# Six low-word roundings moved from ScalarE to VectorE, another order of the weight halves, and more of the output stored by column halves

## The chip, the cores and the metric

The program runs on one core of a Trainium2 chip. The metric is the device time of one execution in microseconds, as a median over timed runs. The engines are named as in the profile: PE is TensorE (matmuls; PEld its weight loads), DVE is VectorE, ACT is ScalarE, POOL is GpSimd and SP is the engine that issues the DMAs here.

## The reference, cut to what matters

```
x (8 batches, 8 heads, 512 tokens, 64), state (8, 8, 32, 64)
1. attention  a  = softmax(x @ state^T / 8);   xread = a  @ state
              a2 = softmax(state @ x^T / 8);   sread = a2 @ x
   out = concat([xread, sread])  ->  8 * 544 rows of 512
2. feed-forward  g = silu(rows @ w_in), rows = g @ w_out       (512 -> 2048 -> 512)
3. soft mixture  logits = rows @ phi                            (32 slots)
   dispatch = softmax over the rows; slot inputs = dispatch^T @ rows
   8 experts (relu(in @ w1[e]) @ w2[e]), 4 slots each
   out = softmax over the slots @ slot outputs                  (4352 x 512)
```

`moe_w_in` and `moe_w_out` are float64: each number is two 32-bit words, a high and a low one, and the kernel makes float32 numbers of them on the chip.

## The kernel before, in words

**Work and stages.** Eight batches of 512 tokens are the blocks k = 0 to 7; the 256 rows that belong to the states of all batches are block 8 (`NB`). For a block, `hid` makes sixteen tiles h (j = 0 to 15) with six fp32r matmuls each; fq = j // 4 says which fourth of the 2048 hidden columns a tile belongs to. For it the block's state rows are multiplied into that fourth of w_in (`wb`, the tiles wbp and wb), and the attention weights are the other operand (`ar`). ACT applies silu into a tile g, DVE transposes it into `blk_t[k]`, and `logits` multiplies it with `w2p`, which is the product of w_out's fourth and phi. There are six g buffers, and `logits` frees them. `s_dTg` (tiles S) gathers the slot sums of a block later. After block 8 the slot inputs go through w1 (tiles f) and w2 (tiles so), and `out_tiles` makes the output (tiles o).

**Conversion.** w_in and w_out^T come in sixteen halves of 1 MB (`raw`): four fourths of each, two halves per fourth, in the order of the list `halves`: both halves of a fourth of w_in, then both of the same fourth of w_outT. Eight halves are requested at the start (four in each of two large buffers), the others as `conv` frees a place in the second buffer. `conv` turns a half into float32 in four steps: ACT `activation` Prelu on the high words; ACT `activation` Identity on the low words into `part` (the low words are every second word of the raw half); DVE shift by three in place; POOL integer add of the two. `win_half` converts a half of w_in; `wo_half` a half of w_outT, and after the second one two small matmuls (w2ps, w2q) make `w2p` of that fourth. In the first block the calls are: `win_half` of fourth 0 around the first attention, `wo_half` of fourth 0, and then for each next fourth both halves of w_in and both of w_outT.

**Order of the work.** Nothing is issued when the Python code runs: a recorder keeps all operations, and `schedule` plans them with costs that it gives each one (`cost`). At each step an engine takes, among the operations that can start within `LOOK` of the earliest, the one with the smallest `prio`: its place in the recorded order plus a shift plus an entry of the table `RANK`. PE has a rule more: it stays among operations of its present tiling mode (full 128x128 against row- or column-tiled) as long as the best of them is not behind by more than `STAY` or `KEEP`. The planned order of each engine is what is issued. DMAs are operations on SP and are ordered the same way.

**The end.** w1 and w2 (32 MB) come in 32 loads (`load_w`) into buffers as they become free. w2 is loaded by column halves: eight loads for columns 0 to 255, then eight for 256 to 511. As soon as the first column half of the slot outputs is there, `out_tiles` makes columns 0 to 255 of the first `HALVES` = 3 batches and stores them (512 KB each, rows of 1 KB); later, batches 0 to 2 get their second halves, and batches 3 to 7 and the states' rows are made with 512 columns at a time and stored in rows of 2 KB, the states' rows last (two DMAs from 32 partitions each).

```
        if ch == 0:

            for q in range(HALVES):
                out_tiles(q, slice(0, 256), sets[0])
    for q in range(NB + 1):
        out_tiles(q, slice(256 if q < HALVES else 0, 512), sets[(q + HALVES) % 2])
```

Of the kernel before, what the change touches and what calls it, by code (L numbers as in the profile page):

```python
# [25 lines left out]

BY_PE = (NB,)

WIN = (2, 6)
WIN8 = (0, 2)  # L30

# [6 lines left out]

EVICT = 100

HALVES = 3

# [1 line left out]


RANK = {
    ("0", "ACT", "activation", "acc", 0): 8,
    ("0", "ACT", "activation", "part", 12): 8,  # L50
    ("0", "ACT", "activation", "win", 3): 13,
    ("0", "ACT", "copy", "wb", 2): 71,
    ("0", "DVE", "tensor_scalar", "acc", 0): -9,
    ("0", "DVE", "tensor_scalar", "asm", 3): 120,
    ("0", "DVE", "tensor_tensor", "wb", 0): 459,
    ("0", "DVE", "tensor_tensor", "wb", 3): 126,
    ("0", "DVE", "transpose", "blk", 7): -36,
    ("0", "DVE", "transpose", "s", 4): -40,
    ("0", "PE", "matmul", "lg", 5): 58,
    ("0", "PE", "matmul", "lg", 7): -81,  # L60
    ("0", "PE", "matmul", "wq", 3): -125,
    ("0", "PE", "transpose", "eT", 2): 59,
    ("0", "PE", "transpose", "srT", 1): -75,
    ("7", "DVE", "tensor_reduce", "m", 0): 434,
    ("7", "PE", "matmul", "h", 0): -39,
    ("7", "PE", "matmul", "h", 8): -120,
    ("7", "PE", "matmul", "lg", 5): 30,
    ("7", "PE", "matmul", "wbp", 1): 76,
    ("8", "DVE", "scalar_tensor_tensor", "fin", 0): 68,
    ("8", "PE", "matmul", "S", 3): 155,  # L70
    ("8", "PE", "matmul", "f", 9): 165,
    ("8", "PE", "matmul", "f", 13): 120,
    ("8", "PE", "matmul", "h", 17): 166,
    ("8", "PE", "matmul", "lg", 6): 120,
    ("8", "PE", "matmul", "so", 4): 51,
    ("8", "PE", "transpose", "gt", 8): 71,
    ("8", "PE", "transpose", "hT", 3): -134,
    ("8", "PE", "transpose", "lT", 0): 120,
    ("m", "ACT", "activation", "m", 0): 698,
    ("m", "DVE", "tensor_scalar", "asm", 1): 28,  # L80
    ("m", "PE", "matmul", "S", 2): -150,
    ("m", "PE", "matmul", "h", 5): -324,
    ("m", "PE", "matmul", "lg", 8): -96,
    ("m", "PE", "matmul", "lg", 9): -50,
    ("m", "PE", "transpose", "lT", 0): 416,
}


# [35 lines left out]
class Recorder:  # L124
# [90 lines left out]
    def cost(self, op, eng, what, outs, ins, kwargs):  # L215

        def n(v):
            r = 1
            for s, c in list(v.ap)[1:]:
                r *= c  # L220
            return r

        ps = bass.MemoryType.PSUM
        most = max(n(v) for v in outs + ins)
        pin, pout = any(v.space == ps for v in ins), any(v.space == ps for v in outs)
        strided = any(list(v.ap)[-1][0] > 1 and list(v.ap)[-1][1] > 1 for v in outs + ins)
        if eng == PE:
            lhs, rhs = kwargs.get("lhsT"), kwargs.get("rhs")
            if what == "transpose":
                op.mode, op.tail = FULL, 0.2  # L230
                op.cost += 0.11
                return
            rows, cols = list(lhs.ap)[0][1], n(lhs)
            op.mode = (128 if rows > 64 else 64 if rows > 32 else 32, 128 if cols > 64 else 64 if cols > 32 else 32)
            N = n(rhs)
            if op.mode == FULL:
                split = rhs.dtype == F32R
                op.cost += N / 2.4e3 + 0.0212 if split else max(0.2, 4 * N / 2.4e3 + (0.021 if N > 256 else 0.04))
                op.tail = 0.165
            else:  # L240
                tiles = (128 // op.mode[0]) * (128 // op.mode[1])
                m = 2 * len(op.calls)
                op.cost = max(m / tiles * 2 * N / 2.4e3, m * 0.0135) + (0.07 if tiles == 16 else 0.0068 * tiles)
                op.tail = 0.165
        elif eng == ACT:
            f = kwargs.get("func")
            base = 0.833e-3 * most
            if f in (AF.Abs, AF.Sign, AF.Relu):
                lat = base + (0.26 if pin else 0.29)
            elif len(ins) > 1 and most < 1024:  # L250
                lat = base + (0.258 if pin else 0.285)
            else:
                lat = base + (0.16 if pin else 0.205)
            if kwargs.get("accum_out") is not None:
                op.cost, op.tail = lat + 0.096, 0.0
            else:
                op.cost, op.tail = lat - 0.105, 0.105
            op.mode = {AF.Exp: "e", AF.Silu: "s", AF.Tanh: "es"}.get(f)
        elif eng == DVE:
            sb = [kwargs[x] for x in ("in0", "in1") if x in kwargs and kwargs[x].space == bass.MemoryType.SB]  # L260
            fast = not pin and not pout and what in ("tensor_scalar", "tensor_copy")
            op.port = len(sb) > 1 or fast
            if what == "transpose":
                lat = 0.165 + most / 0.96e3
            elif what == "reciprocal":
                lat = 0.165 + max(0, most - 4) * 6.7e-3
            elif fast:
                lat = 0.262 + most / 1.92e3
            else:
                lat = (0.205 if pin and len(ins) > 2 else 0.155) + most / 0.96e3  # L270
            op.cost, op.tail = lat - 0.08, 0.0 if fast else 0.08
        elif eng == POOL:
            lat = 0.2 + most * 2.135e-3
            if most == 1024:
                lat = 2.39 if outs[0].dtype == F32R else 1.94
            op.cost, op.tail = lat - 0.042, 0.042
        else:
            b = 4
            for s, c in list(outs[0].ap):
                b *= c  # L280
            op.bytes = b
            op.cost = 0.42
# [19 lines left out]
    def schedule(self):  # L302
# [37 lines left out]
        while n_left:  # L340
            best = None
            for e in avail:
# [20 lines left out]
                    continue  # L363
                t_e = min(c[0] for c in cands)
                cands = [c for c in cands if c[0] <= t_e + LOOK[e]]
                pick = min(cands, key=lambda c: (c[1].prio, c[0]))
                if e == PE and mode is not None:
                    near = [c for c in cands if (c[1].mode == FULL) == (mode == FULL)]
                    if near:
                        near = min(near, key=lambda c: (c[1].prio + SAME * (change(c[1]) > 0.2), c[0]))  # L370
                        if near[1].prio <= pick[1].prio + (STAY if mode == FULL else KEEP):
                            pick = near
                if best is None or pick[0] < best[0]:
# [79 lines left out]
        return lambda *a, **k: self._rec.record(self._eng, what, call, a, k)  # L453


LOOK = {PE: 0, DVE: 0.302, ACT: 0.098, POOL: 0.05, SP: 0.0}
DMA_RATE = 405e3
FULL = (128, 128)
STAY, KEEP, SAME = 60, 60, 30


@with_exitstack
def tile_state_attention_soft_moe(
# [65 lines left out]

    raws = [unit("blk", [4, 1024, 2], f"raw{i}", U32) for i in range(2)]  # L530
    n_raw = [0]
    halves = [(kind, f, x) for f in range(4) for kind in ("win", "wo") for x in range(2)]

    def raw_at(n):
        return raws[0][:, n] if n < 4 else raws[1][:, n % 4]
# [7 lines left out]
        src = {"win": w_in, "wo": w_outT}[kind][fq, half].bitcast(U32)  # L543
        nc.sync.dma_start(out=raw_at(n).rearrange("p a b -> p (a b)"), in_=src)

    def conv(raw, dst, r):


        v = raw.rearrange("p (c f) b -> p c f b", f=dst.shape[-1])
        lo, hi, d, r = v[..., 0], v[..., 1], dst.bitcast(U32), r.bitcast(U32)  # L550
        nc.scalar.activation(out=dst, in_=hi.bitcast(F32), func=AF.Prelu, scale=2.0**-112, alpha=2.0**32)
        nc.scalar.activation(out=r, in_=lo, func=AF.Identity, scale=2.0**-29, bias=ulps)
        nc.vector.tensor_scalar(out=d, in0=d, scalar1=3, scalar2=None, op0=ALU.logical_shift_left)
        nc.gpsimd.tensor_tensor(out=d, in0=d, in1=r, op=ALU.add)

# [23 lines left out]

    def wo_half(fq, half):  # L580

        n = 4 * fq + 2 + half
        conv(raw_at(n), acc[:, 2 * half:2 * half + 2], share(half))
        if n >= 4:
            next_raw()
        if half == 0:
# [11 lines left out]
        nc.scalar.mul(out=w2p[:, fq].rearrange("p i s -> p (i s)"), in_=p[:, 0:128], mul=-0.5)  # L598

    def win_half(fq, half):  # L600
        n = 4 * fq + half
        conv(raw_at(n), win_t[fq][:, :, 256 * half:256 * half + 256], share(half))
        if n >= 4:
            next_raw()

# [49 lines left out]
    def a_split(b):  # L655
# [4 lines left out]
        p = at[b, "sc"]  # L660
        for h2 in range(2):
            nc.scalar.copy(out=e[:, 0, h2, :], in_=p[h2])
            nc.vector.transpose(out=s[:, 0, h2, :], in_=e[:, 0, h2, :])
        nc.vector.reduce_max(out=sm[:, 0:2], in_=e[:, 0], axis=AX.X)
        nc.vector.tensor_scalar(out=sm[:, 2:4], in0=sm[:, 0:2], scalar1=-SCALE, scalar2=None, op0=ALU.mult)
        at[b, "tm"] = tm = rot.tile([128, 32, 2], F32, tag="tm", name=f"tm{b}")
# [477 lines left out]
    win_half(0, 1)  # L1144
    a_soft1(0)
    wb(0)
    a_soft2(0)
    a_soft3(0)
    wo_half(0, 0)
    wo_half(0, 1)  # L1150
    load_xT(1)
    a_eT(0, 0)
    a_eT(0, 1)
# [8 lines left out]
    for k in range(NB):  # L1162
# [4 lines left out]
        for j in range(16):  # L1167
# [6 lines left out]
                logits(*divmod(4 * k + fq - 1, 4))  # L1174
                nc.shift = 0
            if k == 0 and i == 0 and fq < 3:
                win_half(fq + 1, 0)
                win_half(fq + 1, 1)
                wo_half(fq + 1, 0)
                wo_half(fq + 1, 1)  # L1180
            if k > 0:
                if j == 1:
                    nc.shift = -FIRST
# [191 lines left out]
    for ch in range(2):  # L1375
# [16 lines left out]
        nc.vector.tensor_copy(out=sor[:, 256 * ch:256 * ch + 256], in_=p[:, 0:256])  # L1392
        if ch == 0:

            for q in range(HALVES):
                out_tiles(q, slice(0, 256), sets[0])
    for q in range(NB + 1):
        out_tiles(q, slice(256 if q < HALVES else 0, 512), sets[(q + HALVES) % 2])
    for k in range(NB + 1):

        lo, hi = WIN8 if k == NB else WIN if k else (4, 4)
# [51 lines left out]
```

## Time and profile before

| what | value |
|---|---|
| median of 3 runs | 467.94 us (467.29 to 468.88) |
| the profiled execution | 466.55 us, its span 464.0 us |
| PE busy | 414.1 us, 89% of the span |
| DVE, ACT, POOL busy | 296.3, 279.6, 135.5 us |
| granted PE clock, mean | 0.984 |
| HBM read and written | 79.37 MB and 12.06 MB |

The span is the time from the first to the last instruction in the trace; the profiled execution's own time holds 2.55 us around it. Times in the rows below are microseconds from the start of the span, mean durations of one instruction nanoseconds.

### The profile page before, as it was taken

The page shows a single profiled execution, that of the slowest core. Times are in us where ns is not written, and L with a number is a line of the kernel's source. Part 1 is how long each engine was busy: PE and PEld are TensorE (multiplying, and loading weights), DVE is VectorE, ACT ScalarE, POOL GpSimd, SP SyncE. Part 2 cuts the span into 40 slices and gives each one's busy share as a digit, 9 for nine tenths or more (in the row PEclk, how much of TensorE's full clock was granted, in tenths as well). Part 3 has the DMA queues.
Part 4 walks back from the last instruction along what each step waited for, and adds up shares of the span by engine and source line. Part 5 has one row for each costly group of instructions (what it writes and reads, how often), then busy time and mean ns, then how long its engine had stood idle before and what let it go on. Part 6 is the DMA issues. An engine that isn't in the chain of part 4 may idle for free.

```text
span 464.0 us, 12243 instructions
## 1 busy us (share of the span) xinstructions
PE 414.1 (89%) x5334; PEld 261.6 (56%) x5334; DVE 296.3 (64%) x519; ACT 279.6 (60%) x488; POOL 135.5 (29%) x75
## 2 busy tenths in 40 slices
PE   1177789999999999999999999999999998899870
PEld 0044456667757766865775776676476784334420
DVE  0876774797787797789778778779942424221280
ACT  3799998758586495585757759568457413011170
POOL 2464577224124133222412313421056410000000
PEclk9999999999999999999999999999999999899995
DMA  8998740510602412142060251212385899999898
GB/s 317 425 429 330 297 167 1 184 59 35 229 2 92 150 80 93 54 175 93 1 229 1 92 171 59 93 47 93 131 324 182 311 375 420 398 426 424 324 331 305
DMA packets 19845, 92.20 MB, mean 199 GB/s; under 512 B 1616, under 2 KB 5072, under 8 KB 11344
## 3 DMA queue, kind: packets, MB, share of 16 engines
q1 hardware_dynamic: 19792, 91.43, 51.3%
q8 instruction: 41, 0.67, 0.6%
q14 instruction: 12, 0.10, 0.1%
HBM read 79.37 MB, written 12.06 MB: 197 GB/s over the span
## 4 chain that ended last, share of the span: by engine, by line
PE 78%; ACT 7%; DMA 6%; DVE 3%; POOL 2%; issue 1%; SPq 0%; DVEq 0%; POOLq 0%
PE h L427 41%; PE S L427 8%; PE lg L427 7%; PE wbp L427 6%; DMA place<-in_w_dram 4%; PE f L427 3%; PE sc L427 2%; ACT part L427 2%; DMA xT<-in_xT_dram 2%; PE eT L427 2%; PE sr L427 2%; PE o L427 1%; PE sib L427 1%; POOL win L427 1%; PE dT L427 1%
## 5 line engine op out<-in xcount | busy, mean ns | idle before, releaser
L427 PE MATMUL h<-ar,wb 128*128 128x512 f32 x768 | 190.2, 400 | 2.0 <-ACT g L427 2.0
L427 PEld LDWEIGHTS h<-ar,wb 128*128 128x128 f32 x768 | 141.7, 190 | 41.3 <-issue 6.9
L427 DVE STREAM_TRANSPOSE blk<-g 128x512 f32<-128x512 f32 x128 | 86.4, 693 | 39.1 <-ACT g L427 38.9
L427 ACT ACTIVATE g<-h 128x512 f32<-128x512 f32 x100 | 59.3, 602 | 77.9 <-PE h L427 56.8
L427 POOL TENSOR_TENSOR wb<-wf,wb 128x512 fp32r<-128x512 f32 x28 | 36.6, 1307 | 152.4 <-ACT wf L427 90.2
L427 PE MATMUL wbp<-win,ss 64*32 64x512 f32 x512 | 34.0, 610 | 10.0 <-POOL win L427 10.0
L427 PEld LDWEIGHTS lg<-g,w2p 128*32 128x32 f32 x1152 | 29.1, 109 | 18.9 <-issue 5.7
L427 ACT CAST wb<-wbp 128x512 fp32r<-128x512 f32 x64 | 34.7, 604 | 7.2 <-PE wbp L427 7.2
L427 PE MATMUL lg<-g,w2p 128*32 128x128 f32 x1152 | 39.0, 276 | 0.0
L427 PE MATMUL S<-blk,dT 32*32 32x512 f32 (+1 forms) x1040 | 38.5, 598 | 0.4 <-ACT dT L427 0.4
L427 POOL TENSOR_TENSOR s<-s,tm 128x1024 f32<-128x1024 f32 x12 | 23.3, 1939 | 33.4 <-DVE tm L427 33.4
L427 DVE TENSOR_TENSOR wb<-wbp,wb 128x512 fp32r<-128x512 f32 x36 | 24.3, 681 | 6.4 <-ACT wb L427 6.3
L427 ACT ACT_TABLE_LOAD x21 | 26.9, 1283 | 1.1 <-PEq L1443 0.7
L427 POOL TENSOR_TENSOR win<-win,part 128x1024 uint32<-128x1024 uint32 x8 | 19.4, 2436 | 24.9 <-DVE win L427 8.6
L427 POOL TENSOR_TENSOR wlo<-win,whi 128x1024 fp32r<-128x1024 f32 x8 | 18.9, 2389 | 16.5 <-ACT whi L427 16.5
L427 POOL TENSOR_TENSOR acc<-acc,part 128x1024 uint32<-128x1024 uint32 x8 | 20.5, 2559 | 9.3 <-ACT part L427 4.6
L427 DVE SCALAR_TENSOR_TENSOR g<-thb,h 128x512 f32<-128x512 f32 x28 | 18.2, 677 | 5.7 <-ACT thb L427 5.7
L427 PEld LDWEIGHTS wbp<-win,ss 64*32 64x32 f32 x512 | 7.5, 106 | 24.8 <-POOL win L427 11.8
L427 PE MATMUL h<-whi,rd 128*128 128x512 f32 x64 | 20.7, 404 | 0.0
L427 PEld LDWEIGHTS S<-blk,dT 32*32 32x32 f32 (+1 forms) x1040 | 13.0, 103 | 13.2 <-issue 8.6
L427 DVE SCALAR_TENSOR_TENSOR acc<-acc,m,S 128x512 f32<-128x512 f32 x28 | 19.1, 742 | 2.0 <-PE S L427 2.0
L427 ACT ACTIVATE part<-raw,ulps 128x1024 uint32<-128x1024 uint32 x16 | 20.0, 1256 | 0.0
(151 smaller groups left out, 563.7 us busy)
## 6 DMA issues: line engine op xcount, KB each, us to landing
place<-in_w_dram SPq DMA_DIRECT2D x17, 1024.0 KB, 9.4
blk<-in_w_dram SPq DMA_DIRECT2D x13, 1024.0 KB, 10.0
raw<-in_w_in_dram SPq DMA_DIRECT2D x8, 1024.0 KB, 7.8
xT<-in_xT_dram SPq DMA_DIRECT2D x8, 1024.0 KB, 5.2
raw<-in_w_outT_dram SPq DMA_DIRECT2D x8, 1024.0 KB, 7.8
xk<-in_xk_dram SPq DMA_DIRECT2D x8, 1024.0 KB, 5.0
blk<-in_w_out_dram SPq DMA_DIRECT2D x6, 1024.0 KB, 4.8
wo_f<-blk SPq DMA_DIRECT2D x6, 512.0 KB, 2.7
```

Source lines behind the costliest of these rows:

```text
L427: made = [call(*args, **kwargs) for call, args, kwargs in op.calls]
```

## The change

The low words of six of the sixteen halves (numbers 4, 6, 8, 10, 12, 14 of the list) are rounded by a DVE `tensor_scalar` in place of ACT's `activation`. The halves come in another order: fourths 0 and 1 of w_in, fourth 0 of w_outT, then in turn a fourth of w_in and one of w_outT, with w_outT's last fourth at the end; requests and conversion calls follow it. In the first block's attention DVE transposes the scores from PSUM in place of ACT's copy. At the end `HALVES` becomes a list: the first column halves of batches 0 to 6 and of the states' rows are made and stored as soon as the first half of the slot outputs is there, then the second halves in the same order, and batch 7 last with 512 columns at a time. The planner gets other costs, other `LOOK`, `STAY`, `KEEP` and `SAME`, and another `RANK` table, which holds SP entries too. The diff, with the table cut to the entries for SP:

```diff
+RAW = [("win", 0), ("win", 1), ("wo", 0), ("win", 2), ("wo", 1), ("win", 3), ("wo", 2), ("wo", 3)]
+
+LOW_DVE = (4, 6, 8, 10, 12, 14)
...
-HALVES = 3
+HALVES = (0, 1, 2, 3, 4, 5, 6, NB)
...
+    ("0", "SP", "dma_start", "cst", 0): 94,
+    ("0", "SP", "dma_start", "phi", 0): 249,
+    ("0", "SP", "dma_start", "raw", 2): -6,
+    ("0", "SP", "dma_start", "raw", 4): 243,
+    ("0", "SP", "dma_start", "raw", 6): 86,
+    ("0", "SP", "dma_start", "ss", 1): 274,
...
-LOOK = {PE: 0, DVE: 0.302, ACT: 0.098, POOL: 0.05, SP: 0.0}
+LOOK = {PE: 0, DVE: 0.05, ACT: 0, POOL: 0.05, SP: 0.0}
...
-STAY, KEEP, SAME = 60, 60, 30
+STAY, KEEP, SAME = 447, 423, 284
...
-    halves = [(kind, f, x) for f in range(4) for kind in ("win", "wo") for x in range(2)]
+    halves = [(kind, f, x) for kind, f in RAW for x in range(2)]
...
-        nc.scalar.activation(out=r, in_=lo, func=AF.Identity, scale=2.0**-29, bias=ulps)
+        if low:
+            nc.vector.tensor_scalar(out=r, in0=lo, scalar1=2.0**-29, scalar2=2.0**23, op0=ALU.mult, op1=ALU.add)
+        else:
+            nc.scalar.activation(out=r, in_=lo, func=AF.Identity, scale=2.0**-29, bias=ulps)
...
-            nc.vector.transpose(out=s[:, 0, h2, :], in_=e[:, 0, h2, :])
+            nc.vector.transpose(out=s[:, 0, h2, :], in_=e[:, 0, h2, :] if b else p[h2])
...
-            for q in range(HALVES):
+            for q in HALVES:
                 out_tiles(q, slice(0, 256), sets[0])
-    for q in range(NB + 1):
-        out_tiles(q, slice(256 if q < HALVES else 0, 512), sets[(q + HALVES) % 2])
+    for i, q in enumerate([*HALVES, *(q for q in range(NB + 1) if q not in HALVES)]):
+        out_tiles(q, slice(256 if q in HALVES else 0, 512), sets[(i + 1) % 2])
```

## Rows read from the trace of the kernel before

**Rows 1.** Busy time by stretch: from:to, length, engines (instructions), PE clock, DMA share, GB/s.

```profile
0.00:25.82 25.82, 5.67 (x36) 0.68 (x36) 13.69 (x21) 15.49 (x19) 8.56 (x8) 1.00 0.93 377
25.82:70.00 44.18, 35.12 (x322) 21.78 (x328) 31.92 (x45) 42.82 (x58) 26.96 (x12) 1.00 0.76 295
...
82.00:375.00 293.00, 292.98 (x3832) 198.65 (x3831) 219.82 (x387) 190.69 (x352) 91.35 (x53) 1.00 0.33 123
375.00:437.00 62.00, 57.13 (x752) 28.48 (x751) 15.51 (x40) 11.71 (x25) 0.00 (x0) 0.97 0.99 404
```

**Rows 2.** Chain that ended last: start, length, what.

```profile
1.66 7.20 DMA xT<-in_xT_dram
...
10.99 0.59 ACT e L427
...
25.42 2.37 POOL acc L427
27.83 1.92 PE w2ps L427 x4
29.75 2.86 PE h L427 x6
...
139.18 1.59 PE h L427 x6
...
145.64 11.01 PE h L427 x48
...
416.23 20.70 DMA place<-in_w_dram
```

**Rows 3.** Timeline of PE around the stretch of conversion.

```profile
53.76 1.67 PE L427 MATMUL h<-ar,wb 128*128 128x512 f32 x6 [1.97 <-ACT g L427]
```

**Rows 4.** Groups of ACT between 25.82 and 70: busy, mean ns, idle before.

```profile
L427 ACT ACTIVATE part<-raw,ulps 128x1024 uint32<-128x1024 uint32 x11 | 13.8, 1262 | 0.0
```

**Rows 5.** Groups of DVE over the whole span.

```profile
L427 DVE TENSOR_SCALAR blk<-blk 128x1024 uint32<-128x1024 uint32 x12 | 8.3, 693 | 1.9 <-ACT blk L427 1.9
...
L427 DVE SCALAR_TENSOR_TENSOR blk<-blk 128x1024 f32<-128x1024 uint32 x6 | 7.1, 1178 | 0.0
```

**Rows 6.** Timeline of all engines, 15 to 30: start, length, engine, instruction.

```profile
17.34 2.37 POOL L427 TENSOR_TENSOR win<-win,part 128x1024 uint32<-128x1024 uint32 x1 [7.05 <-DVE asm L427]
...
18.97 0.78 DVE L427 TENSOR_SCALAR tm<-tm 128x32 f32<-128x32 f32 x1
...
25.96 2.90 DVE L427 TENSOR_TENSOR ar<-s,ar 128x1024 fp32r<-128x1024 f32 x1
```

**Rows 7.** Timeline of DVE at 99.

```profile
99.41 0.14 DVE L427 TENSOR_SCALAR tm<-tm 128x32 f32<-128x32 f32 x1
```

**Rows 8.** Timeline of all engines at the end.

```profile
427.96 0.73 PE L427 MATMUL o<-thb,place 32*32 32x256 f32 x32 [0.52 <-DVE thb L427]
...
429.63 15.52 SPq L427 DMA_DIRECT2D out_dram<-place  x7
...
436.97 1.07 PE L427 MATMUL so<-place,blk 128*32 128x256 f32 x16 [0.50 <-DMA place<-in_w_dram]
...
439.75 1.57 PE L427 MATMUL o<-thb,place 32*32 32x256 f32 x64 [0.52 <-DVE thb L427]
```

**Rows 9.** Busy time by stretch at the end, columns as in the first group.

```profile
436.00:438.00 2.00, 1.50 (x28) 0.42 (x16) 0.00 (x0) 0.00 (x0) 0.00 (x0) 1.00 1.08 382
456.00:458.00 2.00, 0.00 (x0) 0.00 (x0) 0.00 (x0) 0.00 (x0) 0.00 (x0) 0.50 1.05 401
460.00:462.00 2.00, 0.00 (x0) 0.00 (x0) 0.00 (x0) 0.00 (x0) 0.00 (x0) 0.50 0.94 226
437.00:440.00 3.00, 1.99 (x36) 0.94 (x51) 0.42 (x1) 0.37 (x1) 0.00 (x0) 1.00 0.73 257
440.00:442.00 2.00, 1.82 (x96) 0.92 (x64) 1.40 (x4) 1.28 (x4) 0.00 (x0) 1.00 0.07 22
442.00:444.00 2.00, 2.00 (x82) 1.07 (x64) 1.34 (x4) 1.17 (x4) 0.00 (x0) 1.00 0.84 282
```

More of the change, by code (lines that the diff above doesn't have):

```diff
@@ L39 @@
 EVICT = 100
-HALVES = 3
+HALVES = (0, 1, 2, 3, 4, 5, 6, NB)
 PE, DVE, ACT, POOL, SP = "PE", "DVE", "ACT", "POOL", "SP"
 RANK = {
[L49 to L85, printed above, removed]
@@ new lines @@
+    ("0", "ACT", "activation", "acc", 2): 106,
+    ("0", "ACT", "activation", "acc", 4): 505,
+    ("0", "ACT", "activation", "e", 3): -244,
+    ("0", "ACT", "activation", "g", 3): 128,
+    ("0", "ACT", "activation", "g", 6): 158,
+    ("0", "ACT", "activation", "g", 8): 214,
+    ("0", "ACT", "activation", "g", 9): 314,
+    ("0", "ACT", "activation", "g", 14): 474,
+    ("0", "ACT", "activation", "win", 6): 85,
+    ("0", "ACT", "activation", "win", 7): -290,
+    ("0", "ACT", "copy", "e", 3): 67,
@@ new lines @@
+    ("0", "ACT", "copy", "wb", 0): 139,
+    ("0", "ACT", "copy", "wb", 4): 93,
+    ("0", "ACT", "copy", "ws", 2): 305,
+    ("0", "ACT", "copy", "ws", 3): -70,
+    ("0", "DVE", "reciprocal", "asm", 1): 311,
+    ("0", "DVE", "tensor_scalar", "acc", 2): 83,
+    ("0", "DVE", "tensor_scalar", "part", 2): 365,
+    ("0", "DVE", "tensor_scalar", "tm", 1): 33,
+    ("0", "DVE", "tensor_tensor", "wb", 2): 130,
+    ("0", "DVE", "tensor_tensor", "wb", 3): 20,
+    ("0", "DVE", "transpose", "blk", 3): 103,
@@ new lines @@
+    ("0", "DVE", "transpose", "s", 1): 43,
+    ("0", "PE", "matmul", "h", 1): 782,
+    ("0", "PE", "matmul", "lg", 4): -116,
+    ("0", "PE", "matmul", "lg", 7): -56,
+    ("0", "PE", "matmul", "wps", 3): 216,
+    ("0", "SP", "dma_start", "cst", 0): 94,
[4 more added lines that the diff above has]
+    ("0", "SP", "dma_start", "ss", 1): 274,
+    ("7", "ACT", "copy", "lg", 0): -113,
@@ new lines @@
+    ("7", "PE", "matmul", "h", 4): 600,
+    ("7", "PE", "matmul", "wbp", 0): -80,
+    ("7", "PE", "matmul", "wbp", 2): -693,
+    ("8", "ACT", "copy", "whi", 0): -371,
+    ("8", "PE", "matmul", "S", 0): -286,
+    ("8", "PE", "matmul", "f", 12): 363,
+    ("8", "PE", "matmul", "f", 15): 534,
+    ("8", "PE", "matmul", "h", 2): 495,
+    ("8", "PE", "matmul", "so", 6): 796,
+    ("8", "PE", "matmul", "top", 1): -426,
+    ("8", "PE", "transpose", "gt", 5): 8,
+    ("8", "PE", "transpose", "hT", 0): -61,
@@ new lines @@
+    ("8", "PE", "transpose", "hT", 2): -627,
+    ("8", "SP", "dma_start", "place", 19): -56,
+    ("m", "ACT", "activation", "cw", 0): 564,
+    ("m", "ACT", "activation", "e", 0): 114,
+    ("m", "ACT", "activation", "e", 1): -78,
+    ("m", "ACT", "activation", "s", 0): 162,
+    ("m", "ACT", "activation", "sums", 0): 450,
+    ("m", "ACT", "activation", "thb", 2): -335,
+    ("m", "ACT", "copy", "e", 0): 462,
+    ("m", "ACT", "copy", "wb", 3): 139,
+    ("m", "DVE", "reduce_sum", "cm", 0): 26,
@@ new lines @@
+    ("m", "DVE", "tensor_scalar", "tm", 0): 294,
+    ("m", "PE", "matmul", "S", 0): -505,
+    ("m", "PE", "matmul", "S", 1): -60,
+    ("m", "PE", "matmul", "h", 3): 70,
+    ("m", "PE", "matmul", "h", 8): -59,
+    ("m", "PE", "matmul", "h", 11): 411,
+    ("m", "PE", "matmul", "lg", 8): -67,
+    ("m", "PE", "matmul", "lg", 9): -446,
+    ("m", "PE", "matmul", "wbp", 1): 143,
+    ("m", "PE", "matmul", "wbp", 2): -422,
+    ("m", "PE", "transpose", "eT", 1): 409,
+    ("m", "PE", "transpose", "srT", 0): 543,
@@ L237, in cost @@
                 split = rhs.dtype == F32R
-                op.cost += N / 2.4e3 + 0.0212 if split else max(0.2, 4 * N / 2.4e3 + (0.021 if N > 256 else 0.04))
+                op.cost += N / 2.4e3 + 0.0157 if split else max(0.2, 4 * N / 2.4e3 + (0.021 if N > 256 else 0.04))
                 op.tail = 0.165
@@ L242, in cost @@
                 m = 2 * len(op.calls)
-                op.cost = max(m / tiles * 2 * N / 2.4e3, m * 0.0135) + (0.07 if tiles == 16 else 0.0068 * tiles)
+                op.cost = max(m / tiles * 2 * N / 2.4e3, m * 0.0135) + (0.07 if tiles == 16 else 0.0068 * tiles - (0.02 if N == 128 else 0.0))
                 op.tail = 0.165
@@ L249, in cost @@
                 lat = base + (0.26 if pin else 0.29)
-            elif len(ins) > 1 and most < 1024:
+            elif most == 1024 and outs[0].dtype == U32:
+                lat = 1.256
+            elif f == AF.Prelu:
+                lat = 1.165
+            elif len(ins) > 1:
                 lat = base + (0.258 if pin else 0.285)
@@ L260, in cost @@
             sb = [kwargs[x] for x in ("in0", "in1") if x in kwargs and kwargs[x].space == bass.MemoryType.SB]
-            fast = not pin and not pout and what in ("tensor_scalar", "tensor_copy")
+            fast = not pin and not pout and not strided and what in ("tensor_scalar", "tensor_copy")
             op.port = len(sb) > 1 or fast
@@ L274, in cost @@
             if most == 1024:
-                lat = 2.39 if outs[0].dtype == F32R else 1.94
+                lat = {F32R: 2.39, U32: 2.5}.get(outs[0].dtype, 1.94)
             op.cost, op.tail = lat - 0.042, 0.042
@@ L365, in schedule @@
                 cands = [c for c in cands if c[0] <= t_e + LOOK[e]]
-                pick = min(cands, key=lambda c: (c[1].prio, c[0]))
+                pick = min(cands, key=lambda c: (c[1].prio, c[0], c[1].idx))
                 if e == PE and mode is not None:
@@ L369, in schedule @@
                     if near:
-                        near = min(near, key=lambda c: (c[1].prio + SAME * (change(c[1]) > 0.2), c[0]))
+                        near = min(near, key=lambda c: (c[1].prio + SAME * (change(c[1]) > 0.2), c[0], c[1].idx))
                         if near[1].prio <= pick[1].prio + (STAY if mode == FULL else KEEP):
@@ L544, in next_raw, with conv @@
         nc.sync.dma_start(out=raw_at(n).rearrange("p a b -> p (a b)"), in_=src)
-    def conv(raw, dst, r):
+    def conv(raw, dst, r, low):
         v = raw.rearrange("p (c f) b -> p c f b", f=dst.shape[-1])
@@ L580, in wo_half @@
     def wo_half(fq, half):
-        n = 4 * fq + 2 + half
-        conv(raw_at(n), acc[:, 2 * half:2 * half + 2], share(half))
+        n = halves.index(("wo", fq, half))
+        conv(raw_at(n), acc[:, 2 * half:2 * half + 2], share(half), n in LOW_DVE)
         if n >= 4:
@@ L600, in win_half @@
     def win_half(fq, half):
-        n = 4 * fq + half
-        conv(raw_at(n), win_t[fq][:, :, 256 * half:256 * half + 256], share(half))
+        n = halves.index(("win", fq, half))
+        conv(raw_at(n), win_t[fq][:, :, 256 * half:256 * half + 256], share(half), n in LOW_DVE)
         if n >= 4:
@@ L1146, in tile_state_attention_soft_moe @@
     wb(0)
+    win_half(1, 0)
     a_soft2(0)
+    win_half(1, 1)
     a_soft3(0)
-    wo_half(0, 0)
-    wo_half(0, 1)
     load_xT(1)
@@ L1176, in tile_state_attention_soft_moe @@
             if k == 0 and i == 0 and fq < 3:
[L1177 to L1180, printed above, removed]
+                for kind, f in RAW[2 * fq + 2:2 * fq + 4]:
+                    for half in range(2):
+                        (win_half if kind == "win" else wo_half)(f, half)
             if k > 0:
```

## The prediction

> **What bounds the kernel now.** I read the busy times by stretch first. Between 82 and 375 us PE is busy 292.98 of 293.00 us: whatever reaches that stretch later or earlier moves the rest with it [rows 1]. The two places where PE is not full are the ends. Up to 25.82 it does 5.67 us of work, and from there to 70 it is busy 35.12 of 44.18 us, so 9.06 us are lost; in that second stretch ACT is busy 42.82 us, 97% of it, DVE 31.92, POOL 26.96 [rows 1]. ACT bounds the conversion, then; a sign of it is the matmul group at 53.76, which waited 1.97 us for a g of ACT [rows 3].
>
> The chain of waits shows how the first h comes about: the transfer of xT until 8.86, then the softmax of the first attention on ACT and DVE, then POOL's add of a half of w_outT at 25.42, a w2ps matmul of 1.92 us at 27.83, and h at 29.75 [rows 2]. At the other end the chain is one transfer, the last weight, from 416.23 to 436.93 [rows 2]. From 375 to 437 the DMA engines are 99% busy at 404 GB/s [rows 1]. These loads start as PE frees their buffers, so they move with PE. After 437 comes a hole: the DMA share is 0.73, 0.07 and 0.84 in the next 3, 2 and 2 us, before the stores of the second halves arrive; then the stores run at 401 GB/s until a last stretch of 226 GB/s [rows 9].
>
> **Part 1: the conversion.** Six roundings leave ACT. Eleven of them in the stretch took 13.8 us, 1.26 us each [rows 4], so ACT loses 6 x 1.26 = 7.6 us of work. DVE gains six `tensor_scalar` of 1024 columns that read every second word. The trace has no such instruction. The nearest are the in-place shift of 1024 packed words, 0.69 us, and a two-operand instruction of the other conversion that reads the same low words, 1.18 us [rows 5]. I take the second, since it has the same strided input: 6 x 1.18 = 7.1 us more on DVE, with 4.1 us as the cheap end.
>
> What hides it: DVE has 44.18 - 31.92 = 12.3 us idle in the stretch. What is gained has three limits: ACT's 7.6 us, PE's 9.06 us, and DVE, whose 31.92 + 7.1 = 39.0 us leave at most 5.2 us to cut from 44.18. The smallest is DVE's 5.2. The new order adds room beside it: with w_in's first two fourths ahead, the second fourth's wb no longer waits behind two halves of w_outT, and the first w2ps no longer stands ahead of the first h. Against it stands one new cost: SP's entry of -6 brings the third request (now a half of w_in's second fourth) up to the second place, ahead of xT. One MB at the 377 GB/s of the first stretch [rows 1] is 2.8 us, by which xT lands later and the first scores with it. Behind the scores stood ACT's copy of 0.59 us, which the transposes from PSUM skip [rows 2], the 1.92 us of w2ps [rows 2], and DVE's subtraction for ar, which took 2.90 us beside POOL's add in place of some 1.2 [rows 2, 5, 6], 1.7 us. These add up to 4.2 us, so that the first h should come no later than before, and up to some 3 us earlier.
>
> All other requests of the start move too: the constants, phi, the rest of the state and one half of w_outT go behind the others on SP. None is needed before the first w2ps or transposes, which come after the first h; if they were late, logits of fourth 0 would be, and the six g buffers would stop h after j = 5.
>
> I take 5.0 us for this part, from DVE's limit, with 0 (DVE's present idle time stays idle, since it is waiting) and 9 us (PE's idle time all filled) as ends.
>
> [...] A one-input DVE instruction of 32 columns at 18.97 took 0.78 us and ended at 19.75, just after POOL's add that ran from 17.34 to 19.71 [rows 6]; with POOL idle the same instruction took 0.14 us [rows 7]. [...]
>
> **Part 2: the order on PE in the blocks.** `STAY`, `KEEP` and `SAME` rise from 60, 60, 30 to 447, 423, 284, so PE changes less often between full and tiled matmuls. A group of six h behind a tiled one takes 1.59 us, against 11.01 / 8 = 1.38 us in a long run [rows 2]: 0.21 us a return. If two returns in three blocks fall away, that is some 0.14 x 6 = 0.8 us in the six middle blocks. I take 0.8, with 3 us at one end (two to three returns a block) and a loss at the other (a rival).
>
> **Part 3: the stores.** The hole between 437 and 444 is 3 x 0.27 + 2 x 0.93 + 2 x 0.16 = 3.0 us of DMA time [rows 9]. Its cause is that only three half batches are there to store until the last weight has passed so, sor and the second o tiles, which begin at 439.75 [rows 8]. With eight groups ahead there are 7 x 0.52 + 0.26 = 3.9 MB of first halves, which at 401 GB/s last 9.8 us from 437. The price on PE is five more o groups of 0.73 us before the last so [rows 8], 3.7 us where PE had about 0.5 us free at 436.97 [rows 8]: the last so and with it the second halves could come 3.2 us later, at about 443, still before 447 when the first halves run out. So the hole closes: 3.0 us. The last DMAs are now those of batch 7 from all 128 partitions in place of the states' 32: the last 2 us carried 226 in place of 401 GB/s [rows 9], 0.9 us of lost transfer, of which I count 0.6. Against it, five more batches and the states go out in rows of 1 KB. The stretch at 436, mostly such rows, has 382 GB/s at share 1.08 against 401 at 1.05 [rows 9], 7% less for a full queue; 5.5 MB or 13.7 us at 4 to 7% is 0.5 to 0.9; I take 0.5. Sum 3.1 us, with 0 and 4 as ends. SP's issues wait on nothing new, since all weights are issued before (the last at 416.23 [rows 2]).
>
> **Sum.** 5.0 + 0.8 + 3.1 = 8.9 us. The profiled execution took 466.55 us, 464.0 of them its span; 466.55 - 8.9 = 457.65. The median of the runs shown is 467.94, 1.39 above the profiled one, so I predict 459.0.
>
> **The rivals.**
> 1. DVE takes over as the bound and the front gives nothing: the roundings wait for POOL. Each add takes 2.37 us [rows 6]; six roundings that each wait for one whole add cost DVE 6 x (0.69 + 2.37) = 18.4 us, more than its 12.3 us idle, and the front would be longer by up to 6 us. Half such waits give about 12 us, and the front stays as it was. For it: the two stalls at 18.97 and 25.96 [rows 6]. Against: POOL is busy only 26.96 of 44.18 us [rows 1], so most meetings are short. Time with a front of zero: 467.94 - 3.9 = 464.0. Chance 0.14; beyond it, a front longer by 2.5 to 5.3 us leaves the kernel within 0.3% of before, chance 0.05.
> 2. The first halves don't come in time or the store queue gains nothing: 467.94 - 5.8 = 462.1. It needs PE to put the o groups behind the so's. For it: PE has only 0.5 us free there [rows 8]. Chance 0.07.
> 3. Slower: the longer stays on PE starve it. In a long run of h PE waits for g once the six buffers are full; the one such wait shown cost 1.97 us [rows 3]. At once a block that is 6 x 1.97 = 11.8 us; with the other gains kept, 467.94 - 8.1 + 11.8 = 471.6. It decides from (8.1 + 1.4) / 6 = 1.6 us a block. Against: PE now has none in 293 us [rows 1], and the planner leaves a mode when nothing in it can start. Chance 0.07.
>
> **How the numbers follow.** The forecast's own case, both ends gaining, has 0.67: its bounds are 467.94 - (9 + 3 + 4) = 452 and 467.94 - 3 = 465. The range of 453 to 465 holds most of it and rivals 1 and 2, and leaves out the rest. About 0.3%, or 1.4 us, is what a measurement of this kernel can tell from no change. Faster 0.87, within 0.06, slower 0.07.
>
> **What would show it.** Between 26 and the point from which PE is full, ACT's share falls below its 97% and DVE's rises from 72% to 85 to 95%; PE is full from about 65 rather than 70 us. The six roundings on DVE show 0.7 or 1.2 us each, with longer ones where an add runs. The first h starts between 26 and 30 us, with xT landing near 11.5. The middle blocks stay at their 38 us each, up to 0.5 less. In the last 27 us the DMA share has no stretch under 0.9 before the end, and the span from the last weight to the end shrinks from 27 to about 24 us. The prediction is wrong if PE shows waits in the middle, if xT's delay reaches the first h, or if the hole stays.

## The result, and the profile after

The changed kernel takes 461.78 us (median of 4 runs, 460.66 to 463.24) against 468.41 us of the kernel before: ratio 0.985 [0.982, 0.989]. A second set of six runs gave 461.38 us and 0.986 [0.983, 0.989]. So it is faster by 6.6 us, or 6.9 in the second set, where 8.9 were forecast; the forecast of 459.0 lies 2 to 3 us low, the range of 453 to 465 holds it.

Two profiles of the changed kernel are read here. The first is of a run of 463.24 us. These are its busy times by stretch (columns as in [rows 1]):

```profile
25.82:70.00 44.18, 38.17 (x349) 24.13 (x349) 36.90 (x52) 39.28 (x57) 26.08 (x11) 0.96 0.76 297
53.10:56.50 3.40, 3.40 (x10) 2.63 (x9) 3.04 (x6) 3.40 (x5) 3.00 (x2) 0.50 0.78 265
...
82.00:375.00 293.00, 293.00 (x3750) 196.02 (x3750) 223.66 (x384) 193.41 (x353) 91.69 (x53) 1.00 0.33 121
375.00:437.00 62.00, 57.43 (x901) 28.11 (x899) 18.65 (x47) 12.10 (x28) 0.00 (x0) 1.00 1.01 410
```

Between 26 and 70 us ACT's share fell from 97% to 89%, DVE's rose from 72% to 84%, and PE's from 79% to 86%. But PE's granted clock is 0.96 of full there, since it was 0.50 from 53.10 to 56.50 us. The second profile, of a run of 461.08 us, has full clock in the same stretch, and it is the one that is compared with the kernel before from here on:

```profile
25.82:70.00 44.18, 38.07 (x355) 23.62 (x356) 41.10 (x54) 40.81 (x58) 27.33 (x12) 1.00 0.75 294
...
100.00:300.00 200.00, 200.00 (x2620) 131.15 (x2619) 161.69 (x274) 136.87 (x254) 61.08 (x37) 1.00 0.28 99
300.00:386.00 86.00, 86.00 (x1022) 61.40 (x1020) 51.48 (x90) 46.49 (x79) 24.91 (x12) 1.00 0.61 231
```

Without the dip of the clock ACT is busy 92% and DVE 93% of this stretch. PE is full in the blocks, as it was. So busy time can't say where the time was gained: the orders of the two kernels differ, and the same tile stands at another place of a block. I therefore counted the matmuls of each tile that had begun by a time T, gave each its mean duration in long runs of the kernel before (h 229 ns, wbp 59, lg 29, S 35, sc 64, eT and dT 148, sr 16, w2ps and w2q 125, and so on), and took the sum from T. That is PE's time lost by T, for idleness or slow matmuls (an estimate; the last five rows are kernels of the experiments):

```
lost by T =                       70    100    200    300    386 us
kernel before                    37.2   37.3   37.7   38.2   42.5
changed, second profile          33.8   34.3   35.4   36.5   39.5
before + roundings on DVE        35.7   42.6   43.0   43.2   47.7
changed, roundings on ACT        39.6   42.4   43.5   44.0   47.8
before + high STAY               37.6   38.6   46.3   55.0   63.6
changed, STAY as before          33.5   37.4   42.6   49.2   52.7
changed, late ranks as before    34.3   35.0   35.7   36.7   44.8
```

Up to 100 us the changed kernel gains 3.0 us. From 100 to 300 it loses 1.3 (2.15 us lost there against 0.87). From 300 to 386 it gains 1.3 (2.98 against 4.27). After that the two chains of waits differ again. First the kernel before, from the middle of block 1 to siT, then the changed one:

```profile
104.25 1.88 PE wbp L427 x32
...
296.00 1.88 PE wbp L427 x32
...
385.89 3.43 PE sia L427 x32
...
394.89 5.21 PE sib L427 x32
...
401.00 1.08 PE siT L427 x8
```

```profile
102.95 1.88 PE wbp L467 x32
...
295.68 1.88 PE wbp L467 x32
...
382.93 3.43 PE sia L467 x32
...
391.80 3.69 PE sib L467 x32
396.39 1.08 PE siT L467 x8
```

Between the two pairs of wbp lie five blocks: 191.75 us before, 192.73 after, so a block now takes 38.55 in place of 38.35 us. From sia to siT it is 15.11 before and 13.46 after, 1.65 us less, nearly all of it in sib. At siT the changed kernel is 4.6 us ahead.

sib has the same 32 matmuls in both. The clock is the difference, as the stretches around it show (columns as before), the kernel before first, each with PE's longest wait ahead of sib:

```profile
393.00:395.00 2.00, 1.09 (x38) 0.81 (x42) 1.27 (x5) 0.14 (x1) 0.00 (x0) 0.90 0.97 390
395.00:397.00 2.00, 2.00 (x12) 0.48 (x16) 0.74 (x5) 0.69 (x1) 0.00 (x0) 0.50 1.09 429
397.00:399.00 2.00, 2.00 (x16) 0.44 (x12) 0.00 (x0) 0.00 (x0) 0.00 (x0) 0.75 1.05 434
...
393.68 0.67 PE L427 MATMUL sibT<-thb,r4e 64*32 64x128 f32 x32 [1.39 <-DVE fin L427]
```

```profile
390.00:392.00 2.00, 1.18 (x38) 0.86 (x42) 1.27 (x6) 0.18 (x1) 0.00 (x0) 1.00 1.01 394
392.00:394.00 2.00, 2.00 (x24) 0.55 (x20) 0.56 (x4) 0.69 (x1) 0.00 (x0) 1.00 1.10 437
...
390.59 0.67 PE L467 MATMUL sibT<-thb,r4e 64*32 64x128 f32 x32 [1.13 <-DVE fin L467]
```

Before, the clock was granted at 0.50 of full when sib began, after a stretch in which PE waited 1.4 us for DVE between two short groups; in 2 us 12 of its matmuls then began where 24 do after the change. After, PE put the `top` matmuls between the two halves of S, its wait is 1.1 us, and the clock stays at 1.00. That the shorter wait kept the clock up is not shown. In the kernel before with only the roundings moved (an experiment below) S and `top` come in the order of the kernel before and the wait is 1.40 us, and still sib takes 3.64 us, as it does after the change:

```profile
398.82 0.67 PE L429 MATMUL sibT<-thb,r4e 64*32 64x128 f32 x32 [1.40 <-DVE fin L429]
...
400.04 3.64 PE L429 MATMUL sib<-wo,sibTs 128*32 128x512 f32 x32 [0.23 <-DVE sibTs L429]
```

### The profile page after: what moved, and what is told of

Its sections match the earlier page's. It is cut to its first block, busy times and chain, and to the rows that moved or that the text cites. A ratio compares the mean times of both kernels' runs of the same rounds, so it can differ in the third digit from the quotient of the medians.

```text
span 461.3 us, 12559 instructions
## 1 busy us (share of the span) xinstructions
PE 416.7 (90%) x5478; PEld 261.3 (57%) x5478; DVE 309.0 (67%) x535; ACT 277.3 (60%) x492; POOL 137.9 (30%) x75
## 4 chain that ended last, share of the span: by engine, by line
PE 77%; DMA 9%; ACT 5%; DVE 4%; POOL 2%; issue 1%; SPq 0%; DVEq 0%; POOLq 0%
PE h L467 43%; PE lg L467 7%; PE S L467 7%; DMA blk<-in_w_dram 7%; PE wbp L467 6%; DMA xT<-in_xT_dram 2%; PE sr L467 2%; PE sc L467 2%; PE o L467 2%; PE eT L467 1%; POOL acc L467 1%; PE dT L467 1%; ACT wb L467 1%; PE sib L467 1%; ACT e L467 1%
## 5 line engine op out<-in xcount | busy, mean ns | idle before, releaser
L467 PE MATMUL h<-ar,wb 128*128 128x512 f32 x768 | 195.4, 406 | 3.8 <-ACT g L467 2.1
L467 DVE STREAM_TRANSPOSE blk<-g 128x512 f32<-128x512 f32 x128 | 88.0, 699 | 22.7 <-ACT g L467 22.3
L467 PE MATMUL lg<-g,w2p 128*32 128x128 f32 x1152 | 41.0, 276 | 0.0
L467 POOL TENSOR_TENSOR win<-win,part 128x1024 uint32<-128x1024 uint32 x8 | 20.9, 2614 | 16.7 <-ACT part L467 10.6
L467 POOL TENSOR_TENSOR ar<-s,ar 128x1024 fp32r<-128x1024 f32 x7 | 16.8, 2406 | 18.7 <-ACT ar L467 18.7
L467 PE MATMUL sc<-xT,ss 64*32 64x512 f32 x128 | 9.6, 658 | 11.7 <-DMA xT<-in_xT_dram 11.7
```

Source lines behind the costliest of these rows:

```text
L467: made = [call(*args, **kwargs) for call, args, kwargs in op.calls]
```

## The experiments

Intervals are 95%; the kernel before ran beside each. Gains and losses in us are worked out from the ratios.

**The changed kernel again** (no edit).

> The changed kernel once more, for a narrower interval and a second profile: in the first one PE's granted clock fell to 0.81 and 0.85 between 50 and 60 us. If that dip is not part of the change, this profile is without it there and its span is about 2 us shorter than 461.3. The ratio to the kernel before stays at 0.985 +- 0.003.

461.38 us, ratio 0.986 [0.983, 0.989]; the span is 459.1 us. The clock's dip is not tied to the change: a trace of a kernel whose front is the one of before (the kernel before with the new stores, in the next experiment) has 0.88 between 26 and 70 us, where the kernel before's own had 1.00. At 100 us the dip has cost the first profile 2.2 us (36.5 lost against 34.3) and that other kernel 1.6 (38.9 against 37.3).

**The stores, taken back and alone.**

```diff
# in the changed kernel
-HALVES = (0, 1, 2, 3, 4, 5, 6, NB)
+HALVES = 3        # and out_tiles' loops of the kernel before
# in the kernel before: the reverse
```

> The changed kernel with the stores of the kernel before (three half batches, the rest with 512 columns). Theory A (both ends gained, the stores 3.1 us as forecast): 3 us slower than the changed kernel, about 465. Theory B (the stores gave about 1 us, as the two profiles read, since the queue runs slower on 1 KB rows): 1 us slower, about 463, and its profile has the hole of 3 us of DMA time after the last weight.

> The kernel before with only the new stores. Theory A: 3 us faster than the kernel before (0.9935). Theory B: 1 us faster (0.998). The front and the blocks are the same in both, instruction for instruction, so the stretch from the last weight to the end can be read alone: 27.1 us in the kernel before; 24 by theory A, 26 by theory B.

463.01 us, 0.989 [0.986, 0.993], and 467.16 us, 0.997 [0.994, 1.000]: 1.7 us lost by taking the stores back, 1.5 won by them alone, the second barely clear of no change. That is nearer theory B than A. Of each, some 0.7 us lies outside the span, which no trace shows: a run of a kernel with the old stores takes 2.7 us more than its span (median; the kernel before and the changed one with the old stores), with the new stores 2.0. The median spans differ by 1.0 us (460.4 and 459.4) and by 0.7 (465.8 and 465.1). The stretch from the last weight's landing to the end, 27.1 us in the kernel before, is 26.8 with the new stores alone, where A expected 24 and B 26. These are the stretches after the last weight, with the old stores in the changed kernel and then with the new ones:

```profile
435.00:437.00 2.00, 1.51 (x22) 0.56 (x10) 0.00 (x0) 0.37 (x1) 0.00 (x0) 1.00 0.81 278
437.00:439.00 2.00, 1.48 (x65) 0.90 (x64) 0.97 (x3) 0.51 (x2) 0.00 (x0) 1.00 0.05 18
439.00:441.00 2.00, 1.82 (x70) 0.72 (x64) 1.62 (x5) 1.42 (x5) 0.00 (x0) 1.00 0.41 139
...
449.00:451.00 2.00, 0.00 (x0) 0.00 (x0) 0.17 (x1) 0.00 (x0) 0.00 (x0) 1.00 1.05 406
```

```profile
437.00:439.00 2.00, 1.34 (x12) 0.60 (x20) 0.05 (x1) 0.37 (x1) 0.00 (x0) 1.00 0.75 265
439.00:441.00 2.00, 1.82 (x80) 0.66 (x67) 1.81 (x5) 1.28 (x4) 0.00 (x0) 1.00 0.78 259
441.00:443.00 2.00, 1.81 (x91) 0.76 (x82) 1.52 (x5) 1.29 (x4) 0.00 (x0) 1.00 0.79 183
...
447.00:449.00 2.00, 0.53 (x21) 0.47 (x34) 0.00 (x0) 0.00 (x0) 0.00 (x0) 1.00 1.09 379
...
453.00:455.00 2.00, 0.00 (x0) 0.00 (x0) 0.00 (x0) 0.00 (x0) 0.00 (x0) 0.83 0.97 287
```

The hole was 2 x (0.19 + 0.95 + 0.59) = 3.5 us; 2 x (0.25 + 0.22 + 0.21) = 1.4 us of it are left. And the full queue moved 379 GB/s on rows of 1 KB (447 to 449 us) against 406 on rows of 2 KB (449 to 451), 7%; with 287 in the stretch in which I take the states' rows to pass.

**The roundings, taken back and alone.**

```diff
# in the changed kernel
-LOW_DVE = (4, 6, 8, 10, 12, 14)
+LOW_DVE = ()
# in the kernel before: LOW_DVE and conv's branch added, nothing else
```

> The changed kernel with all sixteen roundings on ACT. Theory A (the six roundings moved off ACT are the gain of the front): ACT's share between 26 and 70 us goes back to 97% and the kernel is 4 to 5 us slower than the changed one. Rival (the order of the halves is the gain; the roundings on DVE waited for POOL and cost DVE what ACT saved): within 1.5 us of the changed kernel.

> The kernel before with only the six roundings on DVE (its order of halves, its rank table, its stores). Theory C (the roundings are a gain by themselves, ACT being the bound): 3 us faster than the kernel before, 465. Rival D (the roundings help only with the new order and ranks; in the old plan they wait for POOL in places that the plan does not know): within 1 us of the kernel before, or slower.

Without the six roundings the changed kernel takes 470.35 us, 1.004 [1.002, 1.007]: they are worth 8.7 us in it, more than either theory gave them, with a rank table that was not made for their absence. The kernel before with them alone takes 472.48 us, 1.009 [1.006, 1.013]: there they cost 4.2 us. Five of the six are the same halves there, at other places of the order. Both are read in the front. In the first, ACT does 40.13 us from 26 to 70, 91% and not the 97% that theory A expected, and PE waits for it (total, times, longest):

```profile
PE h L467 <- ACT g L467: 5.0, 2, 4.4
```

In the second, two in-place shifts on DVE stood beside two adds on POOL, and what PE waited for is DVE (timelines of POOL and DVE, and the waits):

```profile
64.00 5.57 POOL L429 TENSOR_TENSOR win<-win,part 128x1024 uint32<-128x1024 uint32 x2 [3.98 <-DVE win L429]
```

```profile
64.44 5.68 DVE L429 TENSOR_SCALAR acc<-acc 128x1024 uint32<-128x1024 uint32 x2
```

```profile
PE sc L429 <- DVE wb L429: 3.6, 1, 3.6
PE h L429 <- DVE wb L429: 3.0, 1, 3.0
```

Two shifts of some 0.7 us took 5.68 us, until POOL had ended at 69.57, and DVE's subtractions for wb stood behind them. The clock is below full in both traces between 26 and 70 us (0.93 and 0.96), so a part of what they lose there is the dip's. The planner does not know of such waits in the changed kernel: its `cost` counts a rounding, as `strided`, as 1.22 us that never meets POOL. A plan made with the wait in its costs was not tried.

**STAY, KEEP and SAME, alone and taken back.**

```diff
-STAY, KEEP, SAME = 60, 60, 30        # in the kernel before
+STAY, KEEP, SAME = 447, 423, 284
# in the changed kernel: the reverse
```

> The kernel before with only STAY, KEEP and SAME raised. As forecast in part 2 of the sum, fewer changes between full and tiled matmuls: the blocks take 38.2 us in place of 38.35 and the kernel is 1 us faster. Rival: PE stays too long where the rank table was not made for it, and h waits for g: slower by 1 to 5 us.

> The changed kernel with STAY, KEEP and SAME as before. In the old plan the high values alone cost 23 us. If the rank table was fitted to the high values, so that neither goes without the other: slower than the changed kernel by 3 us or more, with waits of PE in the blocks. If the values matter little once the table is new: within 1.5 us.

491.09 us, 1.048 [1.045, 1.052], and 476.23 us, 1.016 [1.012, 1.020]: 22.7 us slower and 14.3 us slower than the changed kernel (0.986). Each kernel needs the values that its rank table was made with. In the first, between 100 and 300 us, PE waits in the blocks (total, times, longest):

```profile
PE eT L427 <- DVE cw L427: 3.2, 4, 0.8
PE lT L427 <- ACT dT L427: 3.2, 4, 0.8
PE dT L427 <- ACT d L427: 2.5, 4, 0.6
```

These are transposes that need a result just made by another engine: PE stays among full matmuls and has nothing else of that mode to do. In these 200 us it goes back from tiled to full matmuls 14 times, in the kernel before 22 times. The waits are 8.9 of the 16.4 us lost there; the rest was not traced. In the second, PE waits 5.6 us in the same 200 us, 3.2 of them with h for a g.

**xT requested before the third half.**

```diff
-    ("0", "SP", "dma_start", "raw", 2): -6,
```

> The changed kernel without SP's entry of -6: xT is requested ahead of the half of w_in's second fourth again. Theory C: the entry's price is on the path of the first h: xT lands some 2.5 us earlier, the first h with it, and the kernel gains 1 us or less of it, because what follows is bound by ACT and DVE. Rival E: no change within 0.5 us, or slower by up to 2 us, since the half that was brought forward fed ACT in the stretch in which it would else stand idle.

460.03 us, 0.983 [0.980, 0.987], not told apart from the changed kernel by these intervals. Two timelines of PE say why so little comes of it, the changed kernel's and then this one's:

```profile
11.27 1.96 PE L467 MATMUL sc<-xT,ss 64*32 64x512 f32 x16 [11.27 <-DMA xT<-in_xT_dram]
...
29.50 2.50 PE L467 MATMUL h<-ar,wb 128*128 128x512 f32 x5 [0.46 <-DVE ar L467]
```

```profile
9.08 1.96 PE L466 MATMUL sc<-xT,ss 64*32 64x512 f32 x16 [9.08 <-DMA xT<-in_xT_dram]
...
28.92 2.50 PE L466 MATMUL h<-ar,wb 128*128 128x512 f32 x5 [0.47 <-DVE ar L466]
```

The scores come 2.19 us earlier, the rest of the first h 0.58.

**Fewer first halves.**

```diff
-HALVES = (0, 1, 2, 3, 4, 5, 6, NB)
+HALVES = (0, 1, 2, 3, 4, 5)
```

> The changed kernel with the first halves of batches 0 to 5 only; batches 6 and 7 and the states' rows are stored in rows of 2 KB at the end, the states last. Two o groups fewer stand between the last so and sor, so the second halves begin some 2 us earlier after the last weight and the rest of the hole (DMA share 0.75 to 0.79 over 6 us, 1.4 us of DMA time) closes. If that rest is what is missing of the forecast 3.1 us: 1 to 1.5 us faster than the changed kernel. If the queue's rate on small rows is what is missing: within 0.5 us.

461.37 us, 0.985 [0.982, 0.989]: no difference. In its profile the hole is nearly gone:

```profile
438.00:440.00 2.00, 1.48 (x63) 0.90 (x64) 0.66 (x2) 0.20 (x1) 0.00 (x0) 1.00 1.09 380
440.00:442.00 2.00, 1.82 (x91) 0.72 (x64) 1.68 (x6) 1.53 (x6) 0.00 (x0) 1.00 0.81 278
...
456.00:458.00 2.00, 0.00 (x0) 0.00 (x0) 0.00 (x0) 0.00 (x0) 0.00 (x0) 0.50 0.78 186
```

but the end is uneven again, with 186 GB/s in its last full stretch, where the states' rows are last.

**The rank entries of blocks 7 and 8.**

```diff
# the 15 entries of "7" and "8" in the changed kernel's RANK
# replaced by the 15 of the kernel before
```

> The changed kernel with the rank entries of blocks 7 and 8 taken from the kernel before (15 of each). The profiles show a gain that the sum had no term for: from the pair of wbp groups at 296 us to siT the kernel before takes 105.0 us and the changed one 100.7. If these entries make it: about 3 us slower than the changed kernel, with sib at 5.2 us in place of 3.7. Rival (the other planner settings make it): within 1 us.

468.77 us, 1.000 [0.998, 1.003]: the entries are worth 6.7 us in the changed kernel, over twice the 3 expected. From 300 to 386 us PE is busy 82.50 of 86.00 us, and its waits for ACT and DVE there make up the rest:

```profile
300.00:386.00 86.00, 82.50 (x925) 58.80 (x927) 48.03 (x84) 46.50 (x77) 25.90 (x13) 1.00 0.51 195
```

sib takes 3.69 us with them too, behind a wait of 1.65 us:

```profile
396.08 0.67 PE L467 MATMUL sibT<-thb,r4e 64*32 64x128 f32 x32 [1.65 <-DVE fin L467]
```

So its slow clock in the kernel before does not come from the late entries alone, nor from the length of the wait; what keeps the clock up was not settled.

**The order of the halves alone.**

```diff
# in the kernel before: RAW, halves, the index n and the order of the calls of the change; nothing else
```

> The kernel before with only the new order of the halves (all roundings on ACT, its rank table, its stores). Theory C now: order and roundings are worth something only together, since the order lets PE run ahead and then waits for ACT: 0 to 4 us slower than the kernel before. Rival: the order alone gives the front's gain of 3 us: 465.

473.76 us, 1.008 [1.004, 1.012]: 3.6 us slower, within what theory C has. Its runs fall in two groups, 469.4 to 471.9 us and 475.6 to 476.8 us, so the size is loose; its profile is of the second group and is not read, so that PE ran ahead and waited for ACT is not shown.

**The two neutral edits together.**

```diff
-    ("0", "SP", "dma_start", "raw", 2): -6,
-HALVES = (0, 1, 2, 3, 4, 5, 6, NB)
+HALVES = (0, 1, 2, 3, 4, 5)
```

> The changed kernel with both edits that looked neutral or better: xT requested ahead of the third half, and six first halves. If their profiles read right (xT first: 1 us; six halves: the hole is closed, and the end comes 1 to 2 us earlier after the last weight): 459.5 to 460.5, 1 to 2 us faster than the changed kernel. If not: within 0.7 us of it.

461.46 us, 0.983 [0.979, 0.987]: within what can be told of the changed kernel. No version was found that is shown to beat it.

## Why the prediction was right, and which of its terms were off

The two gains that were forecast, of the front and of the stores, are there, and the time lies in the range. That it lies near 459.0 is in part luck: the three parts fell short by 2.0, 2.1 and 1.5 us, and 2.95 us that the sum had no term for stood in. Term by term:

**Part 1, forecast 5.0 us, measured 3.0** (lost by 100 us: 37.3 and 34.3). The direction was right: with the roundings back on ACT, 8.1 us more are lost by 100 us, some 2 of them perhaps by the clock's dip, and of the 11.3 us that PE waits between 25 and 100 us there 9.9 end on ACT, against 4.1 of 6.9 in the second profile. What was mis-sized is the price of a rounding on DVE. I took 1.18 us, from a two-operand instruction with the same strided input. The first profile's group of them (least, median and largest ns):

```profile
L467 DVE TENSOR_SCALAR part<-raw x6: 645/1717/2878, 30.4 to 70.6; 128x1024 uint32<-128x1024 uint32 x6
```

and two of the six, one beside an add of POOL and one that began with POOL idle, in the timeline:

```profile
29.83 2.87 POOL L467 TENSOR_TENSOR acc<-acc,part 128x1024 uint32<-128x1024 uint32 x1 [3.28 <-ACT part L467]
...
30.38 2.88 DVE L467 TENSOR_SCALAR part<-raw 128x1024 uint32<-128x1024 uint32 x1
...
53.80 0.65 DVE L467 TENSOR_SCALAR part<-raw 128x1024 uint32<-128x1024 uint32 x1
```

The one that began with POOL idle, at 53.80 between an add that ended at 53.70 and one that began at 54.10, took 0.65 us with its stepped input, where the packed shift took 0.69 [rows 5]. The one beside the add ended 0.56 us after the add did (32.70 and 33.26). Five of the six began while POOL was at work, in this profile, and ended 0.55 to 0.58 us after POOL's instruction; together the six took 10.3 us (11.7 in the second profile) where 7.1 were forecast. So the nearest row was the wrong one to choose. This is rival 1's mechanism, and it took a part of the gain, not all; that it took all of the missing 2.0 us is not shown.

Of the side terms, one failed: ACT's copy of 0.59 us was not skipped. The transpose reads the scores from PSUM now, but it waited for the copy and began 0.64 us after the scores' end at 13.63, as it had before (10.96 and 11.60):

```profile
14.27 0.72 DVE L467 STREAM_TRANSPOSE s<-sc 128x512 f32<-128x512 f32 x1 [3.49 <-ACT e L467]
```

The others held. xT landed at 11.53 (2.13 + 9.40) as forecast. DVE's subtraction for ar took 1.23 us in place of 2.90. The first h began at 28.65 in the first profile and its five other matmuls at 29.91, against 29.75 before [rows 2]: on the whole no later, no earlier. PE was full from 52 us rather than 65, apart from 0.4 us.

**Part 2, forecast 0.8 us of gain, measured a loss of 1.0 to 1.3.** This step failed. The fewer returns did not come: in the five blocks between the two pairs of wbp PE goes back from tiled to full matmuls 20 times in either kernel, four times a block, and it goes over from one tile's matmuls to another's 130 times in place of 100 (counted from the matmuls' order in the traces). A block takes 38.55 in place of 38.35 us. The values by themselves do bring fewer returns but cost 22.7 us, in part by waits of PE for DVE and ACT, which is the mechanism of rival 3 with another releaser. They work only with the rank table that was fitted to them, and a price for one without the other could not be read from the rows of returns. Which of the planner's other settings (`LOOK`, the costs, the entries for the blocks) makes the 0.2 us a block was not tested.

**A term that the sum did not have:** blocks 7 and 8, 1.3 us from 300 to 386 and 1.65 from sia to siT. I costed no rank entry there. It made up for the loss of part 2 and for half of what parts 1 and 3 fell short. But 1.5 of the 1.65 us are the clock in sib (5.21 and 3.69 us), which is not shown to be the change's doing.

**Part 3, forecast 3.1 us, measured 1.5 to 1.7.** Only 0.7 to 1.0 us of that lie in the span; for the 0.7 outside it the sum had no term. In the span the hole closed by 2.1 us, not 3.0. The smaller rows cost more than the 0.5 us that I allowed: 5.5 MB at 379 in place of 406 GB/s take 1.0 us longer. The 0.6 us counted for the states' rows do not show, with 287 GB/s in the middle of the stores now. Two of the signs named for this part did not come: the DMA share is under 0.9 for 6 us after 437, and the stretch from the last weight to the end did not shrink from 27 to 24 us. It is 27.5 us in the second profile, from 431.64 to 459.13. One reason why the hole stays open in part: I put five o groups before the last so and counted PE's time for them, but PE also stood without a releaser in the trace. These are its o groups in the second profile:

```profile
437.66 0.61 PE L467 MATMUL o<-thb,place 32*32 32x256 f32 x2 [1.62 <-issue]
...
448.47 1.80 PE L467 MATMUL o<-thb,place 32*32 32x256 f32 x40 [2.16 <-issue]
```

The first of these stands ahead of sor and so delays every second half. What PE waited for was not found.

**The sum.** Between the two profiles that are compared it is 3.0 - 1.3 + 1.3 + 1.65 us up to siT and 0.2 from siT to the end (62.98 and 62.74 us), 4.9 us together, which is the difference of the spans (464.0 and 459.1); 0.6 more lie outside them, so that the two runs differ by 5.5 us. The medians differ by 6.6 and 6.9. The rest is the run of before that was profiled: it lies 1.8 us under the median of that kernel's later runs (468.3), the second profile's run 0.3 under its own. Of these 23 later runs the seven with a mean granted clock of 0.983 or more have a median of 466.6 us, the sixteen with 0.976 or less one of 468.9, 2.3 us more, so the scatter that goes with the clock is of that size. With 1.6 us for the stores, as the runs have it, the terms add up to 6.25.

**The rivals.** Rival 1 took place in part. Rival 2 (the o groups wait behind the so's) did not: PE put them between. Rival 3 did not take place, because ranks and values came together.

## What to carry to other kernels

In a kernel whose order comes from a planner with fitted ranks, the parts of a change don't add: here order, roundings and stay values each cost 3.6, 4.2 and 22.7 us by themselves, and the whole with its ranks gains 6.6 to 6.9. Only the stores, which stand behind the planned blocks, are worth about the same in both plans (1.5 and 1.7). So cost the plan, not the edits, and when testing a part alone expect to measure the misfit of the ranks too. Before moving a one-input instruction to VectorE, look in the trace for such instructions that end just after a GpSimd one. Here the rounding took 0.65 us where GpSimd was idle when it began and 1.40 to 2.88 us where GpSimd was at work (first profile), so its price was the wait, and it depended on where the plan put it.

## What was not expected of the hardware

A 1024-column `tensor_scalar` on VectorE that reads every second 32-bit word ran as fast (0.65 us, at 53.80 in the first profile) as one that reads packed words (0.69 us) [rows 5]. The granted clock fell to 0.50 of full in the middle of the front in some runs of a kernel and not in others: from 53.10 to 56.50 us in the first profile of the changed kernel, not in the second. And behind a wait of 1.4 us ahead of sib's matmuls, sib took 5.16 us in the kernel before, where the clock was 0.70 over it, and 3.64 in the one with only the roundings moved, so the length of that wait did not decide it.
